# 22 of 28 blocks of the down product by Strassen instead of 20, and all its sums on one engine

## The chip, the cores and the metric

One core of a Trainium2 chip. The metric is the device time of one execution in microseconds (us), lower is better. Each kernel was executed several times on the same chip as the kernel before, and one execution of each was also recorded by the hardware profiler. Engines: PE is TensorE's matrix multiply, PEld its weight load (which overlaps), DVE is VectorE, ACT ScalarE, POOL GpSimd, SP the engine that issues most DMAs.

## The reference

A GEGLU feed-forward layer, everything bf16, with x 2048 x 1024, w_gate and w_up 1024 x 3584, w_down 3584 x 1024:

```python
def reference(x, w_gate, w_up, w_down):
    return (gelu_tanh(x @ w_gate) * (x @ w_up)) @ w_down
```

## The kernel before

The 2048 tokens are worked in two halves. A half has a **gate/up stage** (pairs of 128-column blocks of F, by Strassen; not touched by the change except at its last pair) and a **down stage**, two groups of 512 tokens, which multiplies the hidden values hT by w_down. F has 28 blocks of 128 rows. 2 x NS of them are multiplied by Strassen's seven products m1 to m7, the other 28 - 2 NS blocks plainly. Each product is NS x 2 matmuls of 128 x 128 by 512 columns. m1 and m2 take bf16 operands straight from hT and w_down; m3 to m7 need sums of blocks: s1 to s4 of hT (VectorE or GpSimd, into `s_mem`), t1 to t4 of w_down (into `t_mem`, as fp32r, a 32-bit type that the profile also lists as f32; t2 and t4 come ready from DRAM), and casts of single blocks by ScalarE. Results add up in four pairs of PSUM banks, PB, VB, QB, RB.

```python
    NS = 10
    NKK = (KF - 2 * NS) // WDT          # plain tiles of two blocks: 4
    wd_pool = ctx.enter_context(tc.tile_pool(name="wd", bufs=3))
# ... cut ...
    def s_down(hT, grp, name, i0, i1):  # ... cut ...
        if name in ("s1", "s3"):
            pool(nc.gpsimd.tensor_tensor(out=t, in0=in0, in1=in1, op=op))
        else:
            dve(nc.vector.tensor_tensor(out=t, in0=in0, in1=in1, op=op))

    def load_wd_to(n1):                 # fetch plain tiles up to number n1
        for n in range(len(wd_tiles), min(n1, NWD)):
            k0 = 2 * NS + (n % NKK) * WDT
            wd_sb = wd_pool.tile([P, WDT, D], BF16, name="wd_sb")
            sp(nc.sync.dma_start(out=wd_sb[:], in_=wdv[:, k0 : k0 + WDT, :]))
            wd_tiles.append(wd_sb)

    def down_group(hT, h, grp, then):   # ... cut ...
        def product(name, bset, lhs, rhs, start=False, behind=None, order=plain):
            left_of = [0] * NS
            for i, u in order:
                mm(bset[u], lhs(i, u), rhs(i), start and i == 0, i == NS - 1)
                left_of[i] += 1
                if behind is not None and left_of[i] == 2:
                    behind(i)           # work that may overwrite what the matmul read
            done(name)                  # work given for after this product
# ... cut: m1, m5, m2, m6, m7, then the plain matmuls of PB ...
        product("m3", QB, lsum(0), rsum(1))
        product("m4", RB, lsum(1), rsum(0))
        for step in steps:              # the rest of the plain matmuls
            load_wd_to(base + step[0][0] + 3)
            for kk, b in step:
                plain_mm(kk, b)
                # ... cut: after a bank's last matmul ...
                on_act = b % 2 == (1 if last_grp else 0)
                if on_act:
                    act(nc.scalar.copy(out=dst, in_=banks[b][:]))
                else:
                    dve(nc.vector.tensor_copy(out=dst, in_=banks[b][:]))
                # ... cut: store; the very last one on ScalarE's queue ...
```

The four plain tiles of a group share three buffers: the fourth can be fetched only when the first one's last reader is done, late in the group.

## Time and profile before

| | before |
|---|---|
| time, median of the first 3 runs | 553.32 us (551.94 to 553.59) |
| span of the profiled run | 550.5 us |
| PE busy | 541.3 us, 98% |
| down stage, first half (its first weight load to that of the next half's gate/up) | 91.40 us |
| down stage, second half (its first weight load to the start of the last bank's copy) | 91.23 us |
| from there to the end of the span ("the tail" below) | 4.19 us |

The last three are differences of start times in the timeline: 187.07 to 278.47, 455.08 to 546.31, and 546.31 to 550.5. They cut the kernel at places that the change leaves alone. PE works nearly always; the room is in the number of matmuls and in the few places where PE stands. The lines are in the prediction below.

### The profile page before, as it was taken

Reading aid. Unit: us, or ns where it says so; the run is one execution under the profiler, and the core shown is the slowest. Engines: PE = TensorE matmul, PEld = TensorE weight load, DVE = VectorE, ACT = ScalarE, POOL = GpSimd, SP = SyncE. Lnnn points to the kernel's source line nnn. Section 1 sums busy time; section 2 is a strip of 40 time slices with the busy share of each in tenths; the row PEclk is TensorE's granted clock in tenths of the full one; section 3 lists DMA queues with packets and bytes.
Section 4 is the critical chain, followed back from the end, with each engine's and each line's share of the span. In section 5 each row is a group of like instructions: output and inputs, shape, how many; then the busy total and the mean of one; then the engine's idle time right before and its main releaser. Section 6 shows DMA issues by size and latency. Waiting matters only on the chain.

```text
span 550.5 us, 7066 instructions
## 1 busy us (share of the span) xinstructions
PE 541.3 (98%) x2396; PEld 361.8 (66%) x2441; DVE 293.3 (53%) x355; ACT 245.1 (45%) x426; POOL 320.2 (58%) x248
## 2 busy tenths in 40 slices
PE   8999999999999999999999999999999999999996
PEld 3456777776777667467567767776677775765662
DVE  1714566655665896823644444444444449695402
ACT  2435545555555315117155555555555551502331
POOL 0487777777666804900598766777767763095000
PEclk9999999999999999999999999999999999999999
DMA  9642364462628789589932240405040527617803
GB/s 272 187 140 89 98 210 160 146 219 87 229 79 296 271 279 194 163 287 270 339 119 84 70 144 8 154 0 155 0 154 28 202 83 260 231 38 231 314 29 115
DMA packets 67363, 88.54 MB, mean 161 GB/s; under 512 B 15616, under 2 KB 46336, under 8 KB 67328
## 3 DMA queue, kind: packets, MB, share of 16 engines
q1 hardware_dynamic: 66640, 87.44, 49.4%
q10 hardware_dynamic: 688, 0.66, 0.4%
q8 instruction: 20, 0.33, 0.3%
q14 instruction: 15, 0.12, 0.1%
HBM read 75.50 MB, written 9.44 MB: 154 GB/s over the span
## 4 chain that ended last, share of the span: by engine, by line
PE 96%; DMA 2%; issue 0%; ACT 0%; ACTq 0%
PE bank L366 59%; PE bank L568 32%; PE bank L234 5%; DMA w_mem<-in_w_up_dram 1%; DMA wd_sb<-in_w_down_dram 1%; PE bank L288 0%; ACT o_sb L705 0%; ACTq L157 0%
## 5 line engine op out<-in xcount | busy, mean ns | idle before, releaser
L366 PE MATMUL bank<-t_mem,s_mem 128*128 128x512 f32 x1040 | 255.2, 399 | 0.0
L366 PEld LDWEIGHTS bank<-t_mem,s_mem 128*128 128x128 f32 x1040 | 195.4, 188 | 45.3
L340 POOL TENSOR_TENSOR s_mem<-w_mem 128x512 fp32r<-128x512 bf16 x104 | 125.1, 1222 | 129.1 <-PE bank L366 77.4
L389 DVE TENSOR_TENSOR bank<-bank,m 128x512 f32<-128x512 f32 x104 | 72.8, 700 | 103.3 <-ACT bank L409 91.6
L249 DVE TENSOR_TENSOR hT<-g_sb,bank 128x512 bf16<-128x512 f32 x112 | 76.8, 687 | 65.0 <-ACT g_sb L244 31.2
L244 ACT ACTIVATE g_sb<-bank 128x512 f32<-128x512 f32 x112 | 66.6, 597 | 87.4 <-DVE bank L389 49.9
L366 PE MATMUL bank<-xT,w_mem 128*128 128x512 bf16 x392 | 97.7, 380 | 1.3
L545 POOL TENSOR_TENSOR s_mem<-hT 128x512 fp32r<-128x512 bf16 (+1 forms) x32 | 67.5, 2140 | 53.2 <-PE bank L568 44.7
L568 PE MATMUL bank<-t_mem,s_mem 128*128 128x512 f32 x400 | 96.2, 397 | 0.1
L568 PEld LDWEIGHTS bank<-t_mem,s_mem 128*128 128x128 f32 x400 | 74.8, 188 | 18.1 <-issue 0.9
L568 PEld LDWEIGHTS <-hT 128*128 128x128 bf16 x416 | 39.5, 98 | 50.0 <-issue 4.4
L366 PEld LDWEIGHTS <-w_mem 128*128 128x128 bf16 x416 | 36.7, 98 | 50.5 <-issue 13.3
L495 DVE TENSOR_TENSOR t_mem<-w_mem 128x1024 fp32r<-128x1024 bf16 (+2 forms) x28 | 61.3, 2232 | 5.4 <-ACT s_mem L536 5.0
L340 POOL TENSOR_TENSOR s_mem<-s_mem,w_mem 128x512 fp32r<-128x512 f32 x52 | 61.1, 1194 | 0.0
L340 POOL TENSOR_TENSOR s_mem<-w_mem,s_mem 128x512 fp32r<-128x512 bf16 x52 | 60.0, 1173 | 0.0
L568 PE MATMUL bank<-wd_sb,hT 128*128 128x512 bf16 x244 | 55.1, 379 | 1.2 <-DMA wd_sb<-in_w_down_dram 0.4
L353 ACT CAST s_mem<-w_mem 128x512 fp32r<-128x512 bf16 x52 | 31.9, 615 | 34.0 <-PE bank L366 29.2
L404 ACT COPY m<-bank 128x512 f32<-128x512 f32 x52 | 30.6, 588 | 17.7 <-PE bank L366 17.7
L409 ACT COPY bank<-bank 128x512 f32<-128x512 f32 x52 | 29.6, 570 | 17.0 <-PE bank L366 17.0
L400 ACT COPY bank<-bank 128x512 f32<-128x512 f32 x52 | 29.6, 570 | 14.2 <-PE bank L366 14.2
L568 PE MATMUL bank<-w_mem,hT 128*128 128x512 bf16 x154 | 35.6, 379 | 0.3
L705 ACT CAST o_sb<-bank 128x512 bf16<-128x512 f32 x16 | 9.4, 586 | 56.6 <-PE bank L568 56.6
(31 smaller groups left out, 196.2 us busy)
## 6 DMA issues: line engine op xcount, KB each, us to landing
t_mem<-t_dram SPq DMA_DIRECT2D x40, 512.0 KB, 5.1
w_mem<-in_w_gate_dram SPq DMA_DIRECT2D x11, 1024.0 KB, 5.5
w_mem<-in_w_up_dram SPq DMA_DIRECT2D x11, 1024.0 KB, 7.8
w_mem<-in_w_down_dram SPq DMA_DIRECT2D x10, 1024.0 KB, 7.9
wd_sb<-in_w_down_dram SPq DMA_DIRECT2D x16, 512.0 KB, 3.7
wd_sb<-in_w_down_dram SPq DMA_DIRECT2D x20, 256.0 KB, 7.0
t_dram<-o_sb SPq DMA_DIRECT2D x20, 256.0 KB, 2.0
out_dram<-o_sb SPq DMA_DIRECT2D x12, 256.0 KB, 2.4
```

Of the source, the lines that this page charges most:

```text
L244: act(nc.scalar.activation(out=g_sb[:], in_=ps[:], func=ACT.Gelu_apprx_tanh))
L249: nc.vector.tensor_tensor(out=hT[:, fc, tb * TB : (tb + 1) * TB], in0=g_sb[:], in1=ps[:], op=ALU.mult,)
L340: pool(nc.gpsimd.tensor_tensor(out=t, in0=in0, in1=in1, op=op))
L353: act(nc.scalar.copy(out=t, in_=a(1, 1)))
L366: nc.tensor.matmul(banks[bank][:], lhsT=lhs[:, c, :], rhs=rhs[:, c, :], start=start and c == 0, stop=c == KH - 1, skip_group_check=True,)
L389: nc.vector.tensor_tensor(out=banks[dst][:], in0=banks[src][:], in1=m5[j][:], op=ALU.add)
L400: act(nc.scalar.copy(out=banks[QB[j]][:], in_=banks[PB[j]][:]))
L404: act(nc.scalar.copy(out=m5[j][:], in_=banks[VB[j]][:]))
L409: act(nc.scalar.copy(out=banks[RB[j]][:], in_=banks[QB[j]][:]))
L495: dve(nc.vector.tensor_tensor(out=t, in0=in0, in1=in1, op=ALU.subtract))
L545: pool(nc.gpsimd.tensor_tensor(out=t, in0=in0, in1=in1, op=op))
L568: nc.tensor.matmul(banks[bank][:], lhsT=lhs, rhs=rhs, start=start, stop=stop, skip_group_check=True,)
```

## The change

The intent: multiply two more blocks of F by Strassen (NS = 11), which saves a few matmuls and leaves three plain tiles, as many as there are buffers; and take GpSimd out of the down stage, where its sums slowed VectorE's. All s and t sums now stand on VectorE, each issued "behind" the product that last reads the place it overwrites. To spare VectorE in exchange, ScalarE alone empties the banks, except in the last group. The core, with cuts (moved buffers and the order in the last gate/up pair are left out):

```diff
-    NS = 10
+    NS = 11
@@ s_down
-        if name in ("s1", "s3"):
-            pool(nc.gpsimd.tensor_tensor(out=t, in0=in0, in1=in1, op=op))
-        else:
-            dve(nc.vector.tensor_tensor(out=t, in0=in0, in1=in1, op=op))
+        dve(nc.vector.tensor_tensor(out=t, in0=in0, in1=in1, op=op))
@@ down_group
-        load_wd_to(base + 3)
         product("m1", PB, h_block(0, 0), wd_block(0, 0), True)
 ...
+        load_wd_to(base + 3)
         product("m2", PB, h_block(0, 1), wd_block(1, 0))
 ...
-            steps[-2:] = [
-                [(NKK - 2, b) for b in VB + QB[:1]]
-                + [(NKK - 1, b) for b in PB + VB + QB[:1]]
-                + [(kk, b) for b in QB[1:] + RB for kk in (NKK - 2, NKK - 1)]
-            ]
+            steps = [[(kk, b) for b in OB for kk in range(NKK) if (kk, b) not in early]]
 ...
-        product("m3", QB, lsum(0), rsum(1))
-        product("m4", RB, lsum(1), rsum(0))
+        product("m3", QB, lsum(0), rsum(1), behind=two(next_s1_t3) if more else None)
+        product("m4", RB, lsum(1), rsum(0), behind=two(next_t1) if more else None)
+        if more:
+            for i in range(0, NS, 2):
+                next_s3(i, min(i + 2, NS))
 ...
-                on_act = b % 2 == (1 if last_grp else 0)
-                if on_act:
+                if b % 2 == 1 or not last_grp:
 ...
-                    if b == OB[-1]:
-                        nc.scalar.dma_start(out=out2[...], in_=dst)
-                    else:
-                        sp(nc.sync.dma_start(out=out2[...], in_=dst))
+                    sp(nc.sync.dma_start(out=out2[...], in_=dst))
```

## The prediction

> **What bounds the kernel now.** I read the page's busy line first, then its chain of waits, then the PE rows of the waits view, and last the timeline of the down stage, which alone prices a matmul.
>
> ```profile
> PE 541.3 (98%) x2396; PEld 361.8 (66%) x2441; DVE 293.3 (53%) x355; ACT 245.1 (45%) x426; POOL 320.2 (58%) x248
> PE 96%; DMA 2%; issue 0%; ACT 0%; ACTq 0%
> PE bank L366 59%; PE bank L568 32%; PE bank L234 5%; DMA w_mem<-in_w_up_dram 1%; DMA wd_sb<-in_w_down_dram 1%; PE bank L288 0%; ACT o_sb L705 0%; ACTq L157 0%
> ```
>
> TensorE is the chain for 96% of the span; the down stage, which the change rewrites, is its 32% (L568). VectorE and GpSimd each have over 40% of the span free, so moving work between them matters only where PE stands behind a sum. The waits view names few such places:
>
> ```profile
> PEld bank L568 <- issue: 0.9, 2, 0.4
> PEld bank L568 <- DVE t_mem L495: 0.6, 2, 0.3
> PE bank L568 <- DMA wd_sb<-in_w_down_dram: 0.4, 1, 0.4
> ```
>
> All of what PE waits for in down is under 2 us. The timeline shows how fast it goes otherwise and where it stands; here is the first group of the second half (start, length, engine, instructions), and one m5 and m2 of its second group:
>
> ```profile
> 453.51 5.82 POOL L545 TENSOR_TENSOR s_mem<-hT 128x1024 fp32r<-128x1024 bf16 x2 [0.44 <-PE bank L366]
> ...
> 455.09 4.49 PE L568 MATMUL bank<-w_mem,hT 128*128 128x512 bf16 x19
> 457.28 0.68 DVE L249 TENSOR_TENSOR hT<-g_sb,bank 128x512 bf16<-128x512 f32 x1
> 457.88 2.54 DVE L495 TENSOR_TENSOR t_mem<-w_mem 128x1024 fp32r<-128x1024 bf16 x1
> ...
> 459.23 5.37 PE L568 MATMUL bank<-t_mem,s_mem 128*128 128x512 f32 x20
> ...
> 462.20 0.76 PEld L568 LDWEIGHTS bank<-t_mem,s_mem 128*128 128x128 f32 x4 [0.28 <-DVE t_mem L495]
> 463.21 3.09 DVE L547 TENSOR_TENSOR s_mem<-s_mem,hT 128x512 fp32r<-128x512 f32 x5
> ...
> 464.43 4.49 PE L568 MATMUL bank<-w_mem,hT 128*128 128x512 bf16 x19
> ...
> 468.57 9.46 PE L568 MATMUL bank<-t_mem,s_mem 128*128 128x512 f32 x40
> ...
> 477.88 2.76 PE L568 MATMUL bank<-wd_sb,hT 128*128 128x512 bf16 x11
> ...
> 480.29 9.46 PE L568 MATMUL bank<-t_mem,s_mem 128*128 128x512 f32 x40
> ```
> ```profile
> 504.96 4.91 PE L568 MATMUL bank<-t_mem,s_mem 128*128 128x512 f32 x20
> 509.71 4.49 PE L568 MATMUL bank<-w_mem,hT 128*128 128x512 bf16 x19
> ```
>
> I use start-to-start times, because lengths overlap. m2 (20 bf16) takes 468.57 - 464.43 = 4.14 us, the early plain block (12 bf16, one record missing) 480.29 - 477.88 = 2.41: one more bf16 matmul costs (4.14 - 2.41)/8 = 0.216 us. m6 with m7 (40 fp32r) takes 477.88 - 468.57 = 9.31, an undisturbed m5 (20) 509.71 - 504.96 = 4.75: one more fp32r matmul costs (9.31 - 4.75)/20 = 0.228 us. The first m5 of the half takes 464.43 - 459.23 = 5.20, so 0.45 us were lost behind t1, whose DVE pieces ran at 2.54 us while GpSimd worked. The first half shows the same 0.45.
>
> **What the Trainium skill says.** "TensorE: Matmul & The Clock Gate", section "Wait — 56ns, not 53.3ns?", gives a warm matmul N/2.4 GHz plus about 2.5 ns, 215.7 ns at 512 columns. The bf16 pace of 0.216 agrees; the page prices no fp32r matmul, and 0.228 is this trace's. "VectorE: DVE Perf Modes", section "The TRN2 errata", gives an fp32 tensor_tensor (N+151)/0.96 ns, 691 ns at 512 and 1224 at 1024. The rows have 684 to 700 ns at 512 and a minimum of 1210 at 1024, so it agrees; back to back the trace is a little better (five in 3.09, 0.62 each). "GPSIMD Engine Reference", section "8. Key points", says that GpSimd shares its SBUF interfaces with VectorE and contends with DVE instructions that have two SBUF inputs. The trace agrees strongly: a 1024-column difference takes 2.54 us beside GpSimd against 1.21 alone, and GpSimd's 512-column sum 2007 ns on average in down against about 1200 in the gate/up stage.
>
> **The change part by part.**
> 1. Matmuls. A group of down (four in the program) has 7 x 2 x NS products and 8 plain matmuls for each of the 28 - 2 NS blocks left. NS = 10: 140 + 64 = 204; NS = 11: 154 + 48 = 202. By kind: products m3 to m7 are fp32r, 100 before and 110 after; the rest is bf16, 104 and 92. So a group loses 12 x 0.216 = 2.59 us and gains 10 x 0.228 = 2.28, net -0.31 us; four groups -1.26 us. All of this is on the path.
> 2. GpSimd leaves down. Its s1 and s3 sums go to VectorE, and the sums that stood in front of m5 are no longer slowed. The two 0.45 us at m5 should go: -0.9 us.
> 3. Three plain blocks per group instead of four, and three buffers, so no block of a group is fetched while that group runs its plain part. Before, the fourth tile of the second group stood behind the next half's weights (PE waited 0.43, and the load of weights behind it makes about 0.5 us): -0.5 us.
> 4. VectorE's new load. By the trace's back-to-back rates, 11 blocks of s cost 2816 columns, about 3.4 us (as six instructions), and 11 blocks of t 5632 columns, about 6.5 us. Per group s1 to s4, t1, t3 and four m5 additions make 13.6 + 13.0 + 2.6 = 29 us of a 45 us group: it fits in total. What counts is the order, and the tight place is the first group of a half. I count from m1's start. VectorE finishes the last GELU product at about +1.9, the rest of t1 with s1 at +6.8, s3 at +10.0, s2 at +13.4, t3 at +19.9, s4 at +23.3, and the additions into Q at +24.0 and +24.6. PE wants t1's last piece at +8.4 (m1 4.57, then 16 matmuls of m5), s2 at +14.4, t3 from +19.4 piece by piece, and Q for m3 at 4.57 + 5.2 + 4.57 + 10.2 + 1.55 = +26.1. It is late nowhere, with 1.5 us to spare at Q and as much at t1. In the second group the sums start behind m3: s1 with t3 10.3, t1 6.5, s3 3.4, so t1 is ready near +43.9 against m5 at +49.5. No wait there.
> 5. ScalarE alone empties the banks in three groups: 8 x 0.57 = 4.6 us against 3.5 us of last plain matmuls, but the first banks, which the next m1 wants, come free first. Its b22 cast grows to 11 x 0.53 = 5.8 us, and m3 reads it in order. No wait.
> 6. GELU's output moves into the upper end of w_mem, whose 6 rows of w_down load only after the last product is read (+0.5 to +1.9). 1.5 MB at the 380 to 400 GB/s that the DMA windows show is 4 us, with latency landed by about +6; m2 wants the first of them near +12.
> 7. In the last gate/up pair a 1024-column t1 piece sits in front of VectorE's addition that frees bank R: ready within 0.1 us of when m4 wants it. I allow +0.1 per half.
> 8. The end: the last store goes by the SP queue instead of ScalarE's; either is issued within 0.05 us of the copy. Zero.
>
> Sum: -1.26 - 0.9 - 0.5 + 0.2 = -2.5 us; from 553.3 that is 550.9. I add 0.2 for small semaphore waits among the many finer pieces: **551.1 us**.
>
> **Rivals.**
> - VectorE becomes the bound in the first group of a half. For it: from the last pair to Q it works without a break for some 24 us, and 6% more per instruction uses up the 1.5 us. Against: every duration is measured, and GpSimd is gone. It would cost up to 1.5 us in each half: about 553 to 554.
> - DMA becomes the wait. For it: the first half's down moves up to 400 GB/s, the w_down rows now load later, t2 comes in seven pieces behind them, and the three plain tiles are no longer fetched before m1. Against: these tiles are wanted only at +24.6, and t2's 2.75 MB takes 7 us and m6 starts at +14.4. It would cost 1 to 3 us in one half: 552 to 554.
> - The waits removed are refilled elsewhere (ScalarE's queue holds evacuations behind casts that wait for the next half's weights): only the matmul saving stays, 552.
>
> **Range and chances.** With everything right 550.7; with one rival half true 552.5. I say 549.9 to 553.0 for 8 in 10. The 2% lines are at 542.3 and 564.4: the best case has no 11 us to give, as PE's work shrinks by only 1.26 us and its waits in down are below 2. A slowdown of 11 us needs a repeated stall that no order here shows. Faster by over 2%: 0.005; within 2%: 0.97; slower: 0.025.
>
> **What would show it.** Step 1: 440 fp32r and 368 bf16 matmuls in down, an undisturbed group of 45.0 us against 45.3 (m1 at 4.57). Step 2: the first m5 of a half at 5.2 us for 22 matmuls, with no DVE wait; t pieces of 1024 columns at 1.2 us. Step 3: no PE wait for the plain tiles. Step 4: no PE or weight-load wait for DVE additions or t_mem; if PE's m3 starts later than 26.2 us after m1, VectorE is the bound. Step 7: a gap before m4 of the last pair. Wrong if the waits view shows PE standing over 1 us in down for DVE or DMA, or if the gate/up stage, which I take as unchanged, moves by more than 0.5 us.

## The result, and the profile after

| | before | after |
|---|---|---|
| median of 4 runs each, same rounds | 552.63 us (551.88 to 553.59) | 548.55 us (548.44 to 548.80) |
| span of the profiled run | 550.5 | 546.8 |
| down stage, first half | 91.40 | 89.72 |
| down stage, second half | 91.23 | 90.14 |
| tail | 4.19 | 3.21 |

The ratio is 0.9926, 95% interval 0.9906 to 0.9946, about 4.1 us less. A ratio here and below is the mean time of one kernel's runs over that of the other's of the same rounds, so it is not quite the ratio of the medians quoted. "Within 2%" was right; 551.1 and its range from 549.9 to 553.0 were not: the kernel came out 2.5 us below the number and 1.4 below the range.

A part of the gain lies where no profile looks. The record gives each run's time and its span, from the first to the last instruction. Time less span is 2.08 to 2.22 us in every run of the kernel before and of its variants, before_dve_sums_act excepted, and 1.74 to 1.86 in that one and in every run of the changed kernel and its variants. So about 0.35 of the 4.1 us are gained outside the span. What does it is not shown: after_pool_sums, with GpSimd's sums back, and after_alt_evac, with the old evacuation, have the small figure too.

The busy line and the chain of waits of the changed kernel (compare the first lines in the prediction):

```profile
PE 538.7 (99%) x2390; PEld 364.9 (67%) x2433; DVE 305.4 (56%) x416; ACT 252.8 (46%) x446; POOL 253.4 (46%) x216
PE 97%; DMA 1%; issue 1%; ACT 0%; ACTq 0%
PE bank L368 60%; PE bank L569 33%; PE bank L232 5%; DMA w_mem<-in_w_up_dram 1%; PE bank L290 0%; ACT o_sb L721 0%; ACTq L155 0%
```

GpSimd has 67 us less to do and VectorE only 12 more; the link of 1% to the plain tile's DMA (wd_sb) is gone from the chain, and PE's down stage (now L569) is 33% of a shorter span. Of the rows of the waits view (waiter, releaser: us in all, times, us of the longest) in which TensorE waits in the down stage, one is left. It had a counterpart before, which the prediction didn't show; here is that one, then the changed kernel's:

```profile
PEld L568 <- issue: 4.4, 15, 0.7
```
```profile
PEld L569 <- issue: 3.7, 14, 0.3
```

"issue" means that the weight load waited for nothing that the profile shows. The three rows of the prediction are gone: no wait for VectorE and none for DMA remains. The gate/up stage, taken as unchanged, is: 176.61 us before (278.47 to 455.08) and 176.60 after. The timeline of the first group of the second half (start, length, engine, instructions):

```profile
453.45 4.92 PE L569 MATMUL bank<-w_mem,hT 128*128 128x512 bf16 x21
458.03 5.39 PE L569 MATMUL bank<-t_mem,s_mem 128*128 128x512 f32 x22
463.25 4.92 PE L569 MATMUL bank<-w_mem,hT 128*128 128x512 bf16 x22
467.83 10.37 PE L569 MATMUL bank<-t_mem,s_mem 128*128 128x512 f32 x44
478.27 1.67 PE L569 MATMUL bank<-wd_sb,hT 128*128 128x512 bf16 x7
```

m5 takes 463.25 - 458.03 = 5.22 us for 22 matmuls. Before it took 5.20 for 20, with 0.45 lost behind t1. m1 takes 4.58 for 22. From m6 to the first plain matmul on record are 10.44; of the eight plain ones seven are recorded, so m6 with m7 takes about 10.2. Now the other side, VectorE in the tight place of the first half, where m1 starts at 187.13:

```profile
187.93 0.68 DVE L251 TENSOR_TENSOR hT<-w_mem,bank 128x512 bf16<-128x512 f32 x1
190.60 2.89 DVE L499 TENSOR_TENSOR t_mem<-w_mem 128x1024 fp32r<-128x1024 bf16 x2
196.54 3.43 DVE L548 TENSOR_TENSOR s_mem<-s_mem,hT 128x512 fp32r<-128x512 f32 x6
199.89 6.43 DVE L499 TENSOR_TENSOR t_mem<-w_mem 128x1024 fp32r<-128x1024 bf16 x7
206.24 3.43 DVE L548 TENSOR_TENSOR s_mem<-hT,s_mem 128x512 fp32r<-128x512 bf16 x6
209.58 1.29 DVE L629 TENSOR_TENSOR bank<-bank,m 128x512 f32<-128x512 f32 x2
213.27 10.35 PE L569 MATMUL bank<-t_mem,s_mem 128*128 128x512 f32 x44
```

These are, in order: the last product with GELU's output, the last pieces of t1, then s2, t3, s4, the two additions into Q, and PE's m3 and m4 on Q and R. VectorE runs in one piece from s2 to Q and is done at 210.87, 2.4 us before m3 wants Q. Earlier in the same trace a difference of 1024 columns alone takes 1.22 us, where before it took 2.54 beside GpSimd.

### The profile page after: what moved, and what is told of

Read it like the earlier page. It is cut to its first block, busy times and chain, and to the rows that moved or that the text cites. A ratio compares the mean times of both kernels' runs of the same rounds, so it can differ in the third digit from the quotient of the medians.

```text
span 546.8 us, 7160 instructions
## 1 busy us (share of the span) xinstructions
PE 538.7 (99%) x2390; PEld 364.9 (67%) x2433; DVE 305.4 (56%) x416; ACT 252.8 (46%) x446; POOL 253.4 (46%) x216
## 4 chain that ended last, share of the span: by engine, by line
PE 97%; DMA 1%; issue 1%; ACT 0%; ACTq 0%
PE bank L368 60%; PE bank L569 33%; PE bank L232 5%; DMA w_mem<-in_w_up_dram 1%; PE bank L290 0%; ACT o_sb L721 0%; ACTq L155 0%
## 5 line engine op out<-in xcount | busy, mean ns | idle before, releaser
L368 PE MATMUL bank<-t_mem,s_mem 128*128 128x512 f32 x1040 | 255.2, 400 | 0.0
L368 PEld LDWEIGHTS bank<-t_mem,s_mem 128*128 128x128 f32 x1040 | 195.5, 188 | 45.2
L251 DVE TENSOR_TENSOR hT<-w_mem,bank 128x512 bf16<-128x512 f32 x112 | 76.6, 687 | 63.9 <-ACT w_mem L246 31.1
L246 ACT ACTIVATE w_mem<-bank 128x512 f32<-128x512 f32 x112 | 66.4, 597 | 87.5 <-DVE bank L391 52.7
L569 PE MATMUL bank<-t_mem,s_mem 128*128 128x512 f32 x440 | 104.4, 395 | 0.0
L569 PEld LDWEIGHTS bank<-t_mem,s_mem 128*128 128x128 f32 x440 | 82.6, 188 | 18.4
L569 PEld LDWEIGHTS <-hT 128*128 128x128 bf16 x368 | 34.9, 98 | 43.8 <-issue 3.7
L499 DVE TENSOR_TENSOR t_mem<-w_mem 128x1024 fp32r<-128x1024 bf16 (+2 forms) x54 | 52.5, 1020 | 0.0
L569 PE MATMUL bank<-wd_sb,hT 128*128 128x512 bf16 x184 | 41.4, 379 | 0.5
L569 PE MATMUL bank<-w_mem,hT 128*128 128x512 bf16 x169 | 39.0, 380 | 0.4
L721 ACT CAST o_sb<-bank 128x512 bf16<-128x512 f32 x28 | 14.4, 620 | 43.9 <-PE bank L569 43.9
L548 DVE TENSOR_TENSOR s_mem<-hT 128x512 fp32r<-128x512 bf16 (+3 forms) x36 | 27.8, 804 | 6.6 <-PE bank L368 3.4
```

Source lines behind the costliest of these rows:

```text
L246: act(nc.scalar.activation(out=g_sb, in_=ps[:], func=ACT.Gelu_apprx_tanh))
L251: nc.vector.tensor_tensor(out=hT[:, fc, tb * TB : (tb + 1) * TB], in0=g_sb, in1=ps[:], op=ALU.mult,)
L368: nc.tensor.matmul(banks[bank][:], lhsT=lhs[:, c, :], rhs=rhs[:, c, :], start=start and c == 0, stop=c == KH - 1, skip_group_check=True,)
L499: dve(nc.vector.tensor_tensor(out=t, in0=in0, in1=in1, op=ALU.subtract))
L569: nc.tensor.matmul(banks[bank][:], lhsT=lhs, rhs=rhs, start=start, stop=stop, skip_group_check=True,)
```

## The experiments

Eighteen further runs were made, two of them of the unchanged kernels. In each table "ratio" is against the kernel before, whose medians were 552.4 to 552.9 over 11 or 12 runs. "First", "second" and "tail" are the stretches defined above, from that kernel's trace. All results were correct.

My theory after reading the traces: 1.26 us from matmuls, 0.9 from the waits at m5, and more than I had allowed from the ends, namely the late fourth tile and the last store. The rivals: the gain beyond the prediction comes from ScalarE's evacuation or VectorE's new order; or there is no gain beyond it, and the base was too high.

### The last store and the last group's order

The span's end moved by 1 us more than the down stages explain, so I took the store first, in both directions, and then the order of the last group's plain matmuls.

```diff
# before_sp_store (kernel before)
-                    if b == OB[-1]:
+                    if False:            # so the last store goes by SP
# after_act_store (changed kernel)
+                    if b == OB[-1]:
+                        nc.scalar.dma_start(out=out2[...], in_=dst)
# after_old_last (changed kernel): the order of the last group's steps as before
-            steps = [[(kk, b) for b in OB for kk in range(NKK) if (kk, b) not in early]]
+            steps[-2:] = [ ... as in the kernel before ... ]
# after_act_old_last: both of the last two
# before_wd4_sp: before_sp_store with the fourth buffer of the next experiment
```

> The kernel before, with its very last output store issued from the SP queue instead of ScalarE's queue; nothing else. In the traces the time from the start of the last bank copy to the end of the span is 4.2 us before and 3.2 us after, and the store on ScalarE's queue took 2.6 us to land against 1.7 to 1.8 us on SP. Theory Q (the queue costs it): 0.9 to 1.0 us faster than before, ratio 0.998, end of the span 3.2 us after the last copy starts. Rival S (the tail shrank because the new order of the last plain blocks spreads the stores out): no change, the last store still lands 2.6 us after its issue, as it follows the second-last store by 0.7 us.

> The changed kernel, with the very last store put back on ScalarE's queue. Theory Q: 0.9 to 1.0 us slower than the changed kernel (about 549.5 against 548.55), store landing 2.6 us. Rival S: no change (548.5), landing 1.7 us, as the stores are spread out.

> The changed kernel with the old order of the last group's plain blocks (evacuations crowded into the last 5 us). Theory Q: no change (548.4 to 548.8). Rival S: about 1 us slower (549.5), as eight stores follow one another within 4 us again.

> The changed kernel with both the old order of the last plain blocks and the last store on ScalarE's queue. Each alone left the tail at 3.2 to 3.3 us. If it takes both (the last store on one queue behind seven crowded ones on the other): tail of 3.5 to 4.2 us and 0.3 to 0.9 us over the changed kernel in runs of the same start, 548.7 to 549.3. Rival: 3.2 to 3.3 and 548.4.

| run | median | ratio (95%) | first | second | tail |
|---|---|---|---|---|---|
| before_sp_store | 552.23 | 0.9986 (0.9970 to 1.0001) | 90.85 | 91.25 | 3.25 |
| after_act_store | 548.61 | 0.9925 (0.9909 to 0.9942) | 89.72 | 90.13 | 3.31 |
| after_old_last | 549.18 | 0.9930 (0.9915 to 0.9946) | 89.72 | 90.14 | 3.24 |
| after_act_old_last | 548.75 | 0.9929 (0.9914 to 0.9944) | 89.72 | 90.13 | 3.31 |

The theory that ScalarE's queue by itself costs 0.9 us fell. Putting the store back on it moved nothing, alone or with the old order: 0.9925 and 0.9929 stand beside the changed kernel's own 0.9926. The old order alone moved nothing either (0.9930; its median is higher because three of its six runs started slowly, see "The start"), so rival S fell too. In the kernel before it is not decided: taking the store away from ScalarE gave about 0.8 us (0 to 1.7), and its trace is also shorter in the first half, where the last store cannot act: its fourth plain tile happened to arrive in time.

The cause of the longer tail stays open. The tail is 4.19 and 3.99 us in the two traces of the unchanged kernel before, and 3.2 to 3.5 in every other trace, those of before with the store still on ScalarE included (3.50 with a fourth buffer, 3.35 with the sums on VectorE). What differs is how long the last store takes to land. The pages' lists of DMA issues have its time at the end of the line, here of before and of after_act_old_last, where the same store goes by the same queue:

```profile
out_dram<-o_sb ACTq DMA_DIRECT2D x1, 128.0 KB, 2.6
```
```profile
out_dram<-o_sb ACTq DMA_DIRECT2D x1, 128.0 KB, 1.7
```

It is 2.4 us in the second trace of before, 2.0 with the fourth buffer, 1.8 with the sums on VectorE. No single edit that I tried accounts for it.

### A fourth buffer for the plain tiles

```diff
# before_wd4 (kernel before; one of GELU's four buffers pays for the place)
-    wd_pool = ctx.enter_context(tc.tile_pool(name="wd", bufs=3))
-    g_pool = ctx.enter_context(tc.tile_pool(name="g", bufs=4))
+    wd_pool = ctx.enter_context(tc.tile_pool(name="wd", bufs=4))
+    g_pool = ctx.enter_context(tc.tile_pool(name="g", bufs=3))
# and each of the three calls of load_wd_to fetches one tile further ahead: + 3 becomes + 4
```

> The kernel before with four buffers for the plain blocks of w_down (and three for GELU's output, to make room), so that the fourth block of a group is fetched with the others and not behind the next half's weights. My step 3: PE's 0.43 us wait for that block goes, the second group of the first half takes 45.3 instead of 45.9 us, the whole 0.5 to 0.6 us less than before (ratio 0.999). Rival (the wait is refilled by another late transfer, such as the next half's weights, which now come earlier or later): no change.

> The kernel before with the fourth buffer and the last store on SP: both of the terms that my prediction priced too low are taken out, what is left against the changed kernel are the matmuls (1.3) and m5 (0.9). If the end costs before 0.3 to 0.9 us because the last store on ScalarE's queue meets seven crowded ones on SP: tail of 3.2 us in the trace, fast-start runs near 550.7, and 2.2 us over the changed kernel. Rival (the end is noise and no term): as before_wd4, 551.1, tail 3.5.

> The kernel before, unchanged, looked at once more. Its runs spread from 551.8 to 554.1 us, while the same kernel with a fourth buffer for the plain blocks had 5 of 6 runs within 551.05 to 551.32. Theory V (the wait for the fourth plain block is what varies, and the one trace that I priced it from was a mild case): the excess of this run over 551.1 us shows as PE's wait for that block near 275 us, so that the wait is above 1 us if the run is above 552.8. Rival (the spread has its place elsewhere, such as the start or the last stores): the wait is near 0.4 us again whatever the run's time, and the first or last 15 us differ.

| run | median | ratio (95%) | first | second | tail |
|---|---|---|---|---|---|
| before_wd4 | 551.14 | 0.9972 (0.9957 to 0.9987) | 90.82 | 91.24 | 3.50 |
| before_wd4_sp | 551.54 | 0.9973 (0.9958 to 0.9988) | 90.82 | 91.22 | 3.40 |
| before_again | 553.12 (one run) | none | 91.97 | 91.27 | 3.99 |

The fourth buffer alone is worth 0.0028 x 552.8 = 1.5 us, give or take 0.8. I had priced this at 0.5. It is not all the tile's: in the traces the fourth buffer also goes with a shorter tail. The store by SP on top of it adds nothing; by then the tail was short already (3.50). The second half does not move, as it must: the late tile stood only in the first half, behind the next half's weights.

Why more than 0.5? The row of PE's wait for that tile, in the trace of before on which I had built the prediction:

```profile
275.23 3.61 PE L568 MATMUL bank<-wd_sb,hT 128*128 128x512 bf16 x15 [0.43 <-DMA wd_sb<-in_w_down_dram]
```

The same row of the waits view in a second trace of the same kernel, and then in the changed kernel with NS = 10 (an experiment below, which has four plain tiles and three buffers as well):

```profile
PE bank L568 <- DMA wd_sb<-in_w_down_dram: 1.0, 1, 1.0
```
```profile
PE bank L569 <- DMA wd_sb<-in_w_down_dram: 1.5, 1, 1.5
```

With three buffers the wait was 0 (before_sp_store), 0.43, 1.0, 1.06 (before_dve_sums_act) and 1.51 us. The first half is longer than the clean 90.82 by 0.03, 0.58 and 1.15 us in the three of these with the kernel before's engines (before_sp_store, before, before_again). So PE's stand varies from run to run, and one trace showed one draw of it. But the mean of these three is 0.59, close to my 0.5: the traces alone do not show that the tile costs more.

Where the rest lies, two traces of the kernel before show when set beside before_wd4's (549.0 us of span). The span of 550.5 has 0.58 more in the first half, 0.69 in the tail and 0.26 before the first down stage; that of 551.0 has 1.15, 0.49 and 0.34. So theory V was half right: of 2.0 us that before_again took over 551.1, the tile has 1.15.

### Matmuls, GpSimd and buffers apart

```diff
# after_ns10 (changed kernel): 20 blocks again, four plain tiles in three buffers
-    NS = 11
+    NS = 10
# (pieces that ended at 11 or 22 end at 10 or 20; the last group's old order)
# after_ns10_wd4: the same with four buffers and the changed kernel's last order
# after_pool_sums (changed kernel, NS = 11): s1 and s3 on GpSimd again
-        dve(nc.vector.tensor_tensor(out=t, in0=in0, in1=in1, op=op))
+        if name in ("s1", "s3"):
+            pool(nc.gpsimd.tensor_tensor(out=t, in0=in0, in1=in1, op=op))
+        else:
+            dve(nc.vector.tensor_tensor(out=t, in0=in0, in1=in1, op=op))
```

> The changed kernel with 20 of 28 F blocks by Strassen, as before, and (because four plain blocks deadlock in the new last step with three buffers) the old order of the last plain blocks; all sums stay on VectorE, in the new order. My step 1 prices the eleventh pair of blocks at 0.31 us a group, 1.26 us in all; with four plain blocks the late fourth one comes back too, up to 0.6. So 549.8 to 550.4, that is 1.3 to 1.9 us over the changed kernel. Rival (the matmul count is not what pays, the moves are): within 0.5 us of the changed kernel.

> The changed kernel, its new order and VectorE sums kept, with 20 blocks by Strassen instead of 22 and a fourth buffer so that no plain block comes late. It isolates the eleventh pair of blocks. My step 1: 1.26 us over the changed kernel, 549.8, with the narrow spread of kernels without a late block. Against the kernel before with four buffers (551.1) it then has the VectorE sums, the order and the tail: 1.3 us faster. Rival (the matmul count is worth nothing, as the fp32r products cost more than I priced): 548.5.

> The changed kernel with s1 and s3 back on GpSimd, in the new order. If GpSimd beside VectorE is what slowed the first m5 of a half (my step 2): a 1024-column t piece near 2 us again where both run, waits of PE behind s or t in both first groups, at least 0.45 us each, so 549.5 or more; probably much more, as the new order interleaves each s1 with a t3 and m5 of the next group waits for s1. Rival (the order alone removed the wait, the engine does not matter): 548.5.

| run | median | ratio (95%) | first | second | tail |
|---|---|---|---|---|---|
| after_ns10 | 551.42 | 0.9966 (0.9947 to 0.9985) | 92.06 | 90.80 | 3.40 |
| after_ns10_wd4 | 551.00 | 0.9951 (0.9933 to 0.9968) | 90.38 | 90.80 | 3.30 |
| after_pool_sums | 550.77 | 0.9948 (0.9932 to 0.9965) | 90.21 | 90.64 | 3.28 |

This is the cleanest set, because traces that differ in one thing can be subtracted. after_ns10_wd4 and the changed kernel differ by NS: 90.38 - 89.72 = 0.66 and 90.80 - 90.14 = 0.66, in all 1.32 us for the matmuls, against 1.26 predicted. before_wd4 and after_ns10_wd4 have the same matmuls and both have four buffers, and differ by the sums' engine and order (and by who empties the banks, GELU's place, the last group's order and the last store): 90.82 - 90.38 and 91.24 - 90.80, twice 0.44 us, against twice 0.45 predicted. It lies at the first m5, which takes 5.21 us in before_wd4 and 4.77 in after_ns10_wd4. Putting GpSimd back beside NS = 11 costs twice 0.5 us. Its trace shows the mechanism, here at the first m5 (first GpSimd's sums, then VectorE's piece of t1, then PE's wait):

```profile
186.58 7.25 POOL L549 TENSOR_TENSOR s_mem<-hT 128x1024 fp32r<-128x1024 bf16 x3
...
187.62 2.18 DVE L499 TENSOR_TENSOR t_mem<-w_mem 128x1024 fp32r<-128x1024 bf16 x1
...
197.34 1.63 PE L572 MATMUL bank<-t_mem,s_mem 128*128 128x512 f32 x6 [0.26 <-DVE t_mem L499]
```

The difference takes 2.18 us instead of 1.22, and PE stands for it. after_ns10 was expected at 549.8 to 550.4 and missed by a microsecond: its tile was 1.51 us late, and its profiled run began slowly (see "The start" below). By runs, four buffers at NS = 10 gave only 0.9951 over 0.9966, 0.8 us, less than the 1.68 of the traces; these two intervals overlap, so I take the size from no single pair.

By timed runs the steps stand as a ladder, each against before: before_wd4 0.9972, after_ns10_wd4 0.9951, and the changed kernel 0.9926, 0.9923 and (with its store moved) 0.9925. That is 1.5, then 1.2, then about 1.5 us; predicted were 0.5, 0.9 and 1.3. Of the second step 0.35 lies outside the span; the last one contains slow starts, which four of after_ns10_wd4's six runs had.

### ScalarE alone on the banks, and the sums without the new order

```diff
# after_alt_evac (changed kernel): the evacuation alternates again
-                if b % 2 == 1 or not last_grp:
+                if b % 2 == (1 if last_grp else 0):
# before_dve_sums_act (kernel before): all sums on VectorE and ScalarE alone on the banks,
# but every sum where it stood, none "behind" a product
-        if name in ("s1", "s3"):
-            pool(...)
-        else:
-            dve(...)
+        dve(...)
-                on_act = b % 2 == (1 if last_grp else 0)
+                on_act = b % 2 == 1 or not last_grp
```

> The changed kernel with every second bank of the first three groups evacuated by VectorE again, as before. VectorE's evacuations stand in its queue behind s3 of the next group. By the trace VectorE finishes s3 at 234.06 us while PE reaches the next m1 at 232.1 and its second bank about then: PE should wait some 2.5 us in each first group, about 5 us in all: 553 to 554. The second group of the first half, with no such sums, should not change. Rival (ScalarE alone is a detail): 548.5.

> The kernel before with s1 and s3 moved to VectorE and ScalarE alone evacuating, but in the old order of issue and with 20 blocks. It tells the engine from the order. Theory (the engine is what pays): no contention, the first m5 of a half without a wait, 0.9 us faster than before. Rival (the order is needed too): in the old order s1 and s3 pieces stand before the last t1 pieces in VectorE's queue; counting 0.62 us for 512 and 1.17 us for 1024 columns from 184.3 us on, the last t1 pieces come at 194.6 and 195.7 while m5 wants them at 194.1 and 195.0, so PE loses about 0.8 us there in each half: 0 to 0.8 us slower than before.

| run | median | ratio (95%) | first | second | tail |
|---|---|---|---|---|---|
| after_alt_evac | 555.71 | 1.0046 (1.0023 to 1.0069) | 92.11 | 94.20 | 3.30 |
| before_dve_sums_act | 552.01 | 0.9976 (0.9961 to 0.9992) | 92.19 | 91.55 | 3.35 |

ScalarE's part of the change is not decoration. With VectorE evacuating half of the banks, its queue has the copy behind six pieces of the next group's s3, and PE stands in each half. The waits view, then VectorE's copies in the timeline:

```profile
PE bank L569 <- DVE o_sb L723: 4.5, 2, 2.2
```
```profile
230.59 3.43 DVE L548 TENSOR_TENSOR s_mem<-hT 128x512 fp32r<-128x512 bf16 x6
...
233.93 2.48 DVE L723 CAST o_sb<-bank 128x512 bf16<-128x512 f32 x4
```

Two stands of 2.23 us explain 4.5 us; the run lost about 7 (555.71 - 548.55). The rest is in the weight loads after the second stand:

```profile
503.38 0.54 PEld L569 LDWEIGHTS <-hT 128*128 128x128 bf16 x3 [2.51 <-issue]
504.19 0.15 PEld L569 LDWEIGHTS <-hT 128*128 128x128 bf16 x1 [0.28 <-issue]
...
507.17 2.08 PEld L569 LDWEIGHTS <-hT 128*128 128x128 bf16 x10 [0.28 <-issue]
```

From 504.19 to 507.17 they come 0.427 us apart instead of 0.216: for seven or eight matmuls TensorE ran at half pace, which costs up to 8 x 0.21 = 1.7 us. After the same stand in the first half it did not. The granted clock shows it: 0.50 from 504 to 507 us, and in the kept trace's own clock record 3.41 us at half rate, from 503.83 on. Each of this kernel's four runs lists a mean clock of 0.997, where the changed kernel's list 1.0; 0.003 of 553 us is 1.7 us, so each run had about one such stretch. The Trainium skill, "TensorE: Matmul & The Clock Gate", section "What's actually happening", describes a clock gate that goes to half rate after an idle window of about 3.4 us, windows that run free of the kernel. The half pace of 0.427 agrees with it. That it came after a gap of 2.23 us, in one of two cases, is not told there. The full-rate stretches around it last 146 and 14 times 3.41 us, so windows of that length tile the trace: the one that ended at 503.83 held the whole gap, and the one that ended near 234.2 only 1.7 us of the gap in the first half. That the position decides fits this, but it is an estimate from one trace and not shown.

before_dve_sums_act was to show the engine without the order. In its trace PE waits 0.87 us per half at the first m5:

```profile
PEld bank L565 <- DVE t_mem L495: 1.7, 4, 0.5
```

The second half is 0.32 us longer than before, the first is 92.19, with a tile 1.06 late. So moving the sums alone gains nothing in the trace; the order is what makes it pay. But its timed runs came out 0.24% faster than before, 1.3 us. Two terms outside the down stages can hold most of it: 0.35 us outside the span, and a tail of 3.35 us where the two traces of before have 4.19 and 3.99. So this run does not show that the moved sums gain, nor does one trace settle the sum.

### How much slack VectorE has

```diff
# in the work behind m5 of the first group, t3's six pieces; then once more, into the same places:
-            "m5": [lambda i=i: t_down("t3", i, min(i + 2, NS)) for i in range(0, NS, 2)]
+ after_t3_plus2: range(0, NS, 2), then 0
+ after_slack18:  range(0, NS, 2), then 8, 10
+ after_slack36:  range(0, NS, 2), then 8, 10, 8, 10
```

> The changed kernel with one redundant t3 piece pair (1.2 us of VectorE work) repeated in the first group of each half, right before s4 and the additions into Q. The trace shows those additions done at 210.87 and m3 starting at 213.27: 2.4 us of slack, so no change (548.4 to 548.8) if the tight place is as I drew it. Rival (VectorE is already the bound there): 1.2 us more per half, 551.

> The changed kernel with 1.8 us of redundant VectorE work (t3 for the last three blocks, done a second time) in the first group of each half, before s4 and the additions into Q. m7 reads these blocks last, near 210.3 us, and they are rewritten by 208.1; the additions end at 212.1 and 212.7, m3 wants the banks at 213.3 and 213.5. So no change against the changed kernel in runs of the same start (548.4). If VectorE has no slack there: 1.8 us per half, 552.

> The same with 3.6 us of redundant work. t3 is rewritten by 209.9, the additions into Q end near 213.9 and 214.5 while m3 wants them at 213.3 and 213.5: PE waits 0.7 to 1.2 us before m3 in each half, 549.8 to 550.8 in a fast-start run. If the slack were the 1.5 us of the prediction, 2 us per half, 552.4.

| run | median | ratio | first | second |
|---|---|---|---|---|
| after_t3_plus2 | 550.68 | 0.9955 (0.9936 to 0.9973) | 90.68 | 91.22 |
| after_slack18 | 548.60 | 0.9927 (0.9909 to 0.9946) | 89.72 | 90.13 |
| after_slack36 | 550.66 | 0.9961 (0.9942 to 0.9980) | 90.55 | 90.96 |

The first of these was a badly made test. The repeated piece 0 is the one that m7 reads first, so PE waited for it long before Q could matter (VectorE's t3, then PE's m7):

```profile
199.84 7.57 DVE L499 TENSOR_TENSOR t_mem<-w_mem 128x1024 fp32r<-128x1024 bf16 x8
...
207.56 5.23 PE L569 MATMUL bank<-t_mem,s_mem 128*128 128x512 f32 x22 [0.71 <-ACT bank L647]
```

t3's row ends at 199.84 + 7.57 = 207.41 and m7's begins at 207.56; the releaser named, a copy by ScalarE, ended at the same time. It cost 0.96 us in the first half and 1.08 in the second. Repeating the last pieces instead is the right test: three blocks more for VectorE (about 1.8 us) cost nothing in either half, six blocks cost 0.83 and 0.82, through the additions into Q that m3 waits for:

```profile
215.28 6.93 PE L569 MATMUL bank<-t_mem,s_mem 128*128 128x512 f32 x28 [0.28 <-DVE bank L629]
```

The expected loss was 0.7 to 1.2 per half. At t3's pace (6.43 us for 11 blocks) the six blocks repeated take 3.5 us, so the slack is about 3.5 - 0.8 = 2.7 us, near the 2.4 read above, and not the 1.5 of the prediction. The first rival had no chance.

### The start

The runs of one kernel fall into two groups about 1.3 us apart: the changed kernel again gave 548.36, 548.40, 548.40 and 549.62, 549.78, 550.00.

> The changed kernel, unchanged, as the control of its runs in this call. 548.4 to 548.8 us again, if its narrow spread is its own; no PE wait over 0.3 us in down. If the spread comes from the chip and not from the kernel: as wide as before's, 2 us.

It came out at a median of 549.01, above what was expected, ratio 0.9923 (0.9906 to 0.9940), first 89.73, second 90.14, tail 3.26: the same kernel in all its parts, so the groups must differ elsewhere. They differ in the first 16 transposes of x. The timeline of the changed kernel's start, then that of after_ns10_wd4:

```profile
5.71 1.07 PE L290 MATMUL bank<-ident,w_mem 128*128 128x128 bf16 x16 [1.13 <-DMA w_mem<-in_x_dram]
```
```profile
5.47 1.89 PE L290 MATMUL bank<-ident,w_mem 128*128 128x128 bf16 x16 [0.70 <-DMA w_mem<-in_x_dram]
```

1.89 us for 16 is nearly half the pace, and six traces begin so (after_ns10, after_pool_sums, after_ns10_wd4, before_wd4_sp, after_act_old_last, after_slack36), though the granted clock from 4 to 12 us reads 1.00 in the three of them that I looked up. The kept traces say why it reads so: stretches without a clock record count as 1.00, and the first record, of a full clock, begins at 3.4 to 5.7 us in the fourteen quick traces and at 9.5 to 10.2 us in these six. Until then TensorE had never been at full pace: in the slow traces all nine warm-up matmuls ran at half pace too, in 4.00 us, about 0.43 each against 0.216 later. So a slow start is a full clock that comes late, and not one that the gap took away. In after_slack36 and after_act_old_last the first down stage begins at 188.51 and 188.24, in the changed kernel's trace at 187.13: the loss lies before it. The nine warm-up matmuls end near 4.7 us and x arrives at 5.5 to 5.8, so there is a gap. If the gap is what delays the full clock, more warm-up that reaches over it must end the slow group:

```diff
-    NWARM = 9
+    NWARM = 11        # after_warm11;  12 in after_warm12
-        b = banks[max(i - 1, 0)]
+        b = banks[max(i - 1, 0) % 8]
```

> The changed kernel with 11 warm-up matmuls instead of 9. TensorE idles 0.7 to 1.1 us between the warm-up's end (4.7 us) and the first transpose (5.5 to 5.8); two more matmuls of 0.43 us fill it. If the slow group of runs is a start at half pace after that gap: all runs in the fast group, 548.3 to 548.8, transposes in 1.07 us. Rival (the pace of the start has nothing to do with the gap): half the runs near 549.8 as in the control, where 3 of 6 were.

> The same with 12: the warm-up may now reach past the arrival of x and cost up to 0.4 us. If the gap is the cause: no run near 549.8, all within 548.3 to 549.0. Rival: as before, two groups.

after_warm11 has a median of 548.41 (0.9920, 0.9903 to 0.9937) and after_warm12 one of 548.38 (0.9920, 0.9901 to 0.9939). All 12 runs lie at or below 549.10, while of 32 runs of six kernels with the changed kernel's speed (the changed kernel twice, the two store and order variants and both together, after_slack18) 10 lie above 549.3. The timeline of after_warm12 has no wait left in front of the transposes:

```profile
0.77 5.18 PE L192 MATMUL bank<-const-bfloat16-1.0 128*128 128x512 bf16 x12 [0.77 <-PEq L849]
...
5.79 1.06 PE L290 MATMUL bank<-ident,w_mem 128*128 128x128 bf16 x16
```

Its twelve warm-up matmuls take 0.43 us each, so they still ran at half pace, and the full clock came at 5.73 us, before the transposes. So the slow group is the start, at about 1.3 us in about a third of the runs, and more warm-up ends it. Whether it is the closed gap or only the longer activity that does it, these two runs don't tell. For the gap speaks an estimate from the clock records, whose stretches of full clock are whole multiples of 3.41 us: one such window earlier, the slow traces could have had the full clock at 6.1 to 6.7 us, and a window that ended there held the whole gap. All four runs of the changed kernel at its first measurement were fast starters. Both warm-up versions beat the kernel before, and are as fast as the changed kernel at its best.

## Why the prediction was right or wrong

The class was right, the number 2.5 us too high. The steps that made the kernel faster came as predicted; the step that failed is the end, priced at zero. By the steps:

- **Step 1, matmuls (1.26): right.** 1.32 us by subtracting traces. The changed kernel has 440 fp32r and 368 bf16 weight loads in down, and an undisturbed group takes 232.11 - 187.13 = 44.98 us, against 45.0.
- **Step 2, GpSimd leaves (0.9): right.** 0.88 us by subtracting traces, m5 5.22 us; putting GpSimd back costs 1.0.
- **Step 3, the plain tiles (0.5): the mechanism was right, the wait is gone; the size was one draw.** I read one wait of 0.43 us as the wait's size. Other traces have 0 to 1.5, and the first half of the kernel before lost 0.03, 0.58 and 1.15. The fourth buffer alone gained 1.5 us by timed runs, three times the term, but its trace has a shorter tail as well, and the runs do not divide the two.
- **Step 4, VectorE's order: right that no wait arises**, too careful with the slack. After m1's start t1 was done at +6.4 (predicted +6.8), s2 at +12.8 (+13.4), t3 at +19.2 (+19.9), Q at +23.7 (+24.6), and m3 came at +26.1 as predicted. The slack is 2.4 to 2.7 us, not 1.5.
- **Step 5, ScalarE: right that it makes no wait.** That it is needed was not priced: the alternation would cost 7 us.
- **Step 6, w_down's rows: right.** PE has no DMA wait in down.
- **Step 7 and the allowance for semaphores (+0.4 in all): did not happen.** No gap before m4; the last pair's 24 matmuls there take 5.65 us in both traces.
- **Step 8, the end (0): the step that failed.** I compared when the store is issued and took that for the whole price. The tail went from 4.19 to 3.21 us, 0.98 less, the largest of the gains that I had not priced. It lies in the landing of the last store, 2.6 us before and 1.7 for the last eight after, which step 8 doesn't price. Why it landed later in the kernel before stays open: in the changed kernel the same queue and the same order cost nothing (after_act_store, after_act_old_last).
- **What no step named (0.35):** the part of the time that lies outside the span.
- **The base.** 553.32 was the median of three runs. Rounds of 11 and 12 runs gave 552.4 to 552.9, and the rounds of the comparison 552.63.

The profiled pair shows how the miss adds up, since its times, 552.63 and 548.62 us, are close to the medians:

| term | predicted | in the pair |
|---|---|---|
| matmuls | 1.26 | 1.32 |
| GpSimd leaves | 0.9 | 0.88 |
| plain tiles | 0.5 | 0.58 |
| the end | 0 | 0.98 |
| allowances | -0.4 | 0 |
| outside the span | 0 | 0.35 |
| before the first down stage | 0 | -0.06 |
| sum | 2.26 | 4.05 (measured 4.01) |

The gain was 1.8 us larger than predicted, and 0.7 come from the base. It is one pair: the tile and the tail vary from run to run, so the shares are an estimate. It was also luck that all four runs of the changed kernel started fast (10 of 32 times 1.3 us is about 0.4, what a usual mean has above the fast group). The range was wrong because it was built from the rivals alone, all of which make the kernel slower; it allowed nothing for a term of the gain being larger than one trace showed.

Of the rivals, VectorE as the bound fell by the slack runs; the DMA wait did not appear in the changed kernel, though its NS = 10 form had 1.5 us of it; the refilled wait appeared only where ScalarE's part was undone.

## What to carry to other kernels

A wait for a transfer that is read off one trace is one draw: before pricing its removal, look whether the transfer is ordered behind something whose time varies, and give the term a range on both sides. Compare the ends of a transfer, and not only when it is issued: a tail priced at zero moved by 1 us. Moving work to another engine pays by its place in that engine's queue: the same sums on VectorE gained in one order, waited in another, and cost 7 us when copies stood behind them. A full clock that comes early or late can split a kernel's runs into two groups; here two or three more dummy matmuls ended it.

## What the Trainium skill lacked or had wrong

- "TensorE: Matmul & The Clock Gate", "LDWEIGHTS (loading the stationary operand)": columns over 1.2, which makes about 107 ns at 128 columns. Bf16 weight loads took 98 ns here, fp32r ones 188; the page gives no price for fp32r, neither here nor for the matmul (22 in 5.22 us against 22 bf16 in 4.58).
- The same page, "What's actually happening": half rate after an idle window of about 3.4 us. Here it followed a gap of 2.23 us once in two times, and then held for 3.41 us.
- No page tells of the granted-clock column of these profiles: it counts the time before the first clock record as full. It shows 1.00 for the stretch from 4 to 12 us in traces of slow starts (after_slack36, after_ns10_wd4, before_wd4_sp), where the first record begins only at 9.6 to 10.2 us.
- "GPSIMD Engine Reference", "8. Key points", names the contention with VectorE without a size. Here a 1024-column difference took 2.18 to 3.16 us beside GpSimd (the 3.16 at 454.20 us in before) against 1.22 alone, and GpSimd's own 512-column sum 2.0 us against 1.2.
- "VectorE: DVE Perf Modes", "The TRN2 errata": 691 ns at 512 columns agrees for one instruction alone (684 to 700 here). The page gives no size for a series of them back to back, which takes less: s2's 2816 columns, five instructions of 512 and one of 256, took 3.43 us, where the formula gives 5 x 0.691 + 0.424 = 3.88.
